# Order of the heads in the mixed rows of a two-pass attention backward kernel, and the steps at which their sums over wo are issued

## The chip, the cores and the metric

One core of one Trainium2 chip. The metric is the time of one execution on the device in microseconds (us); the kernel before took 892.82 us, the median of three runs (890.22 to 893.56). TensorE is PE in the profile's lines (PEld its weight loads), VectorE is DVE, ScalarE is ACT, GpSimd is POOL and SyncE is SP. SP and POOL issue the DMAs.

## The reference, cut to what matters

A decoding step of one pre-norm block, B = 2 sequences of one token, forward and backward. D = 640, 32 heads of 128, and a cache of 4096 keys and values per head.

```
q   = layernorm(x) @ wq                         # per head h: q[b,h], 128 wide
s   = K[b,h] @ q[b,h] * scale ; p = softmax(s)  # 4096 scores
o   = p @ V[b,h]                                # 128 wide
h1  = x + concat(o) @ wo
out = h1 + relu(layernorm(h1) @ w1) @ w2
# gradients of x, K, V, wq, wo, w1, w2 for a given grad_out. The two large ones, per (b, h):
go  = wo[h] @ g_h1[b]                           # 128 wide
gV  = outer(p, go)                              # 4096 x 128
dp  = V[b,h] @ go ; gs = p * (dp - dot(o, go)) * scale
gK  = outer(gs, q)                              # 4096 x 128
```

K and V are read (64 MB each in bf16), gK and gV of the same size are written. V is needed twice: for o, and after the MLP and its gradients for dp.

## The kernel before, in words

**First pass.** `p1_iter(i)`, one row i for each pair (b, h), i = 0 to 65, pipelined over three pairs: row i transposes and multiplies K of pair i (PE, `pair_transpose` and `pair_matvec`), forms the softmax weights of pair i-1 (`ep` on ACT) and K times these weights (`pk`, two halves on DVE, L523), and multiplies V of pair i-2 (`m_ps`, L516). It is a generator that yields eight times, k = 0 to 7; other work is put in at these points.

**Second pass.** `p2_iter(j)`, one head per j in the order of the list `turns`: V again (or still there) is transposed and multiplied by go to give dp, `gsp` (L956), and the outer products gV and gK, two halves each on DVE (L945), which are stored. `p2_tail` ends a head: gsp, two halves of gK, the store.

**The plan.** Rows i = 0 to 39 are first pass alone. From i = P2_AT = 40 each even row also starts a head j of the second pass, whose steps are dealt out to this row and the next odd one (MIXED, REST): j = 0 to 11 in rows 40 to 63, j = 12 and 13 in rows 64 and 65. In the even row stand the transposes of V and the first half of gV, in the odd one the second half of gV, gsp and both halves of gK. After row 65 the second pass runs alone, j = 14 to 63. In mixed rows the gradients are stored through the POOL queue (L1016, L1031), afterwards mostly through SP.

**Buffers and loads.** K, V and W tiles (W is V loaded again for the second pass), 1024 KB each, share 13 buffers of the pool `ld`; a few of them move to `g`, from which gK and gV are taken. The last six heads of each sequence are kept (KEPT = 6, 6): their V stays in its buffer from the first pass to the second, and no W is loaded. All loads are one queue, issued in order by `pump` on SP: K(i), V(i-2), then W of the head that the next row of the plan starts. A load takes the buffer that was given back earliest and waits on SP until its last readers are done; everything behind it waits too.

**The second pass's order for b = 0, before.** GROUPS[0] lists groups of heads: (26, 28), (28, 30), (30, 32), then (0, 8), (8, 16), (16, 24), (24, 26). `turns` follows it: the kept heads 26 to 31 are j = 0 to 5 (rows 40 to 51), the loaded heads 0 to 5 are j = 6 to 11 (rows 52 to 63), 6 to 25 follow.

**The sums over wo.** go of a head is 128 rows of wo times the gradient of h1, one DVE instruction each (`ttr`, L711, 0.82 us, output `rows<-wo_t,rows`). `go_group` makes the sums of one group, and then a chain of short instructions: two on DVE (L734, L736), `pair_rows` (four matmuls on PE, four copies on DVE, L395), the matmuls of `d_ps` (L741, L745), five more on DVE (L747 to L753). It is part of `middle_gen(0)`, which waits in the background queue `bg` and is advanced by `bg_step` after each yield of a row. `slot` says how many sums may be issued at this yield, a credit of 0.2 per yield (RATES[2]) is spent at 0.9 per sum and 0.5 per finished wait, and `wait(n)` lets n times `spread` yields pass (spread is 2 in mixed rows). In mixed rows a sum may be issued at k = 6 of every row and at k = 1 of rows without a head (the odd ones). Before a row with head j starts, `bg_until` issues at once whatever is still missing for that head's go.

Of the kernel before, what the change touches and what calls it, by code (L numbers as in the profile page):

```python
# [15 lines left out]
def kernel(  # L16
# [23 lines left out]
    _, H, Sk, Dh = A_k_cache.shape  # L40
# [13 lines left out]
    GH = 8  # L54
# [14 lines left out]
    def sm(name, dt, *dims):  # L69

        n = 1
        for d in dims:
            n *= d
        words = n if dt == FP32 else -(-n // 2)
        if name not in scr_at:
            scr_at[name] = scr_at.get(None, 0)
            scr_at[None] = scr_at[name] + words
            assert scr_at[None] <= NSCR, (name, scr_at[None])
        ap = scr[:, scr_at[name]:scr_at[name] + words]
        if dt != FP32:  # L80
            ap = ap.bitcast(dt)[:, 0:n]
        if len(dims) == 2:
            ap = ap.rearrange("p (a b) -> p a b", a=dims[0])
        return ap
# [79 lines left out]
    at_k = [1]  # L164
    spread = [1]
    forced = [False]

    def wait(n):

        end = step[0] + n * spread[0]  # L170
        while step[0] < end and not forced[0]:
            yield 0.0
        yield
# [196 lines left out]
    def wo_of(h, c0, c1):  # L370
        return wo_t[h // WH][:, (h % WH) * D + c0:(h % WH) * D + c1]
# [75 lines left out]
    KEPT = (6, 6)  # L447
    GROUPS = []
    for b in range(B):
        first = H - KEPT[b]  # L450
        if b == 0:
            GROUPS.append([(h, h + 2) for h in range(first, H, 2)] + [(h, min(first, h + GH)) for h in range(0, first, GH)])
        else:
            GROUPS.append([(first, H)] + [(h, min(first, h + WH)) for h in range(WH * ((first - 1) // WH), -1, -WH)])
    turns = [(b, h) for b in range(B) for h0, h1 in GROUPS[b] for h in range(h0, h1)]
    turn_of = {bh: j for j, bh in enumerate(turns)}
    kept = {(b, h) for b in range(B) for h in range(H - KEPT[b], H)}
    u_bank = [None]
# [249 lines left out]
    def ttr(in0, in1, acc, width, kc=128, junk=None):  # L708
        if junk is None:
            junk = junk_row  # L710
        nc.vector.tensor_tensor_reduce(out=junk[0:kc, 0:width], in0=in0, in1=in1, scale=1.0, scalar=0.0,  # L711
                                       op0=ALU.mult, op1=ALU.add, accum_out=acc)

    slot = [99]

    def turn():

        while slot[0] <= 0:
            yield 0.0
        slot[0] -= 1  # L720

    def one(src, b):
        return src[:, :, b]

    def go_group(b, h0, h1, hbc):

        hs = slice(h0, h1)
        n = h1 - h0
        go32 = sm("go32", FP32, GH)
        for k in range(n):  # L730
            yield from turn()
            ttr(wo_of(h0 + k, 0, D), hbc, go32[:, k:k + 1], D)
            yield 0.9
        nc.vector.tensor_copy(out=goc[:, hs, b], in_=go32[:, 0:n])  # L734
        pr = sm("pr", FP32, GH)
        nc.vector.tensor_tensor(out=pr[:, 0:n], in0=goc[:, hs, b], in1=OU[:, b, hs], op=ALU.mult)  # L736
        yield from wait(2)
        pair_rows(gom, goc, hs, slice(b, b + 1))
        yield from wait(2)
        d_ps = pst([128, 2, GH], FP32, "mid", "d_ps")  # L740
        nc.tensor.matmul(d_ps[:, 0, 0:n], lhsT=ones_f32, rhs=pr[:, 0:n], start=True, stop=True)  # L741
        for k in range(n):
            h = h0 + k
            MT, side, slot_mt = MTs.pop((b, h))
            nc.tensor.matmul(d_ps[:, 1, k:k + 1], lhsT=MT, rhs=goc[:, h, b:b + 1], start=True, stop=True)  # L745
            mt_free[side].append(slot_mt)
        nc.vector.tensor_scalar(out=negdot[:, hs, b], in0=d_ps[:, 0, 0:n], scalar1=-1.0, scalar2=None, op0=ALU.mult)  # L747
        ud = sm("ud", FP32, GH)
        nc.vector.tensor_tensor(out=ud[:, 0:n], in0=Uc[:, hs], in1=negdot[:, hs, b], op=ALU.mult)
        mg = sm("mg", FP32, GH)  # L750
        nc.vector.tensor_tensor(out=mg[:, 0:n], in0=d_ps[:, 1, 0:n], in1=rt[:, b, hs], op=ALU.mult)
        nc.vector.tensor_tensor(out=ud[:, 0:n], in0=mg[:, 0:n], in1=ud[:, 0:n], op=ALU.add)
        nc.vector.tensor_scalar(out=GQc[:, hs, b], in0=ud[:, 0:n], scalar1=SCALE, scalar2=None, op0=ALU.mult)  # L753
        for h in range(h0, h1):
            done.add(("go", b, h))
        yield
# [470 lines left out]
    P2_AT = H + 2 + M0_ITERS  # L1227
# [4 lines left out]
    i = j = 0  # L1232
# [51 lines left out]
    def p2_whole(j):  # L1284
        yield from p2_iter(j, 0)
        yield from p2_tail(j)
# [8 lines left out]
    for n, (i, j) in enumerate(plan):  # L1295
        all_go = all(("go", B - 1, h) in done for h in range(H))
        if i is None and plan[n - 1][0] is not None:
            pkp.release()
            big1 = tc.alloc_tile_pool(name="big1", bufs=1)
            for _ in range(2):  # L1300
                more_home("ld", big1)
            share(ld=KEPT[1] + 4, g=5)
        if ("w1", B - 1) in done:
            for t in range(NWO):
                if t not in late and all(("go", B - 1, h) in done for h in range(t * WH, min(H, (t + 1) * WH))) and \
                        (t < NWO - 1 or all_go):
                    late[t] = ("g", "g", "g", "q", "q", "q")[len(late)]
                    more_home(late[t], wop, f"wo{t}")
        lq, ll, lg = [sum(v == tag for v in late.values()) for tag in ("q", "ld", "g")]
        if fin is not None and not bg2 and not bg3:  # L1310
            share(ld=4, g=12 + 6 * (lq > 0))
        elif fin is not None and j >= H + KEPT[1] - 1:
            share(ld=4 + ll, g=7 + lg, f=3, q=2 + lq)
        if j is not None:
            while g2 is not None:
                p2_step()
            if j < NP1:
                bg_until(("go", *turns[j]))
            if i is not None and n + 1 < len(plan) and plan[n + 1][1] is None:
                g2 = p2_whole(j)  # L1320
            else:
                g2 = p2_iter(j, 0, 8 if i is None and j <= H else 0, nc.sync if i is None else None)
        if i is None and ("w1", 1) in done and fin is None:
            wts.release()
            fin = tc.alloc_tile_pool(name="fin", bufs=1)
            big2 = tc.alloc_tile_pool(name="big2", bufs=1)
            more_home("f", big2)
            banks.update(sps=[2, 3], o=[4, 5, 6])
            bg2.append(("fin", fin_gen(fin)))
            bg3.append(("gx", gx_gen(fin)))  # L1330
        if i == 12:
            bg.append(("ga", ga_gen()))
        if i == H + 2:
            banks["bc"].insert(0, banks["sps"].pop(0))
        elif i == P2_AT:
            banks["bc"].remove(7)
            banks["sps"].insert(0, banks["bc"][0])
            banks["bc"] = [7]
        rate = RATES[0 if i is not None and i <= H + 1 else 1 if j is None and i < P2_AT else
                     2 if i is not None else 3 if j <= H else 4]  # L1340
        if i is None:
            spread[0] = 2
            at_k[0] = 1
            k = 0
            while g2 is not None:
                p2_step()
                pump()
                slot[0] = int(k in ((1, 3, 5) if j <= H else (1, 4)))
                k += 1
                bg_step(0, rate)  # L1350
                bg_step(1, RATE2 * (0.4 if spreading[0] else 1.0))
                bg_step(2, RATE3)
            continue
        at = MIXED if j is not None else REST
        for k, _ in enumerate(p1_iter(i, i < H + 1, 0)):
            for _ in range(at.get(k, 0)):
                if g2 is not None:
                    p2_step()
            if k == 5:
                a_heads(i)  # L1360
            pump()

            spread[0] = 1 if i < P2_AT else 2
            at_k[0] = k
            if i >= P2_AT:
                slot[0] = int(k == 6 or (k == 1 and j is None))
            elif i > H + 1:
                slot[0] = {1: 2, 3: 1, 4: 1, 6: 1}.get(k, 0)
            else:
                slot[0] = int(k in (1, 6))  # L1370
            bg_step(0, rate)
            bg_step(1, 0.0)
        if i is not None and i in (H + 1, NP1 + 1):
            bg.append((f"m{i // H - 1}", middle_gen(i // H - 1)))
# [42 lines left out]
```

## Time and profile before

| | |
|---|---|
| median of three runs | 892.82 us (890.22 to 893.56) |
| the profiled execution | 893.07 us, its span 891.3 us |
| busy | PE 750.6 us (84%), DVE 685.0 (77%), ACT 487.1 (55%), POOL 155.8 (17%) |
| moved | 361.87 MB, mean 406 GB/s |
| loads | K 64, V 64, W 52 tiles of 1024 KB on SP |
| stores of gK and gV | 101 tiles on SP, 27 on POOL |
| sums over wo (L711, 128x640 from wo_t) | 64, 52.4 us, 818 ns each |
| chain that ended last, by engine | PE 44%, DVE 25%, DMA 11%, ACT 9%, issue 8% |

The page cuts the span into 40 slices of 22.3 us; digits are tenths, and the line of GB/s is what the DMA engines moved in each. A row of a timeline gives the start in us, the duration, the engine, the line in the kernel, the operation with output and inputs, and in brackets how long the engine idled before it and what released it. In the table of stretches the columns are busy time and number of instructions of PE, PEld, DVE, ACT and POOL, then the granted clock of PE, the DMA share and GB/s.

### The profile page before, as it was taken

What the parts mean: (1) busy time and instruction counts of PE and PEld (TensorE: products, weight loads), DVE (VectorE), ACT (ScalarE), POOL (GpSimd) and SP (SyncE); (2) the same over time, 40 slices, a digit from 0 to 9 for tenths busy, and PEclk for the clock granted to TensorE, in tenths of its full rate; (3) what the DMA queues carried; (4) which work ended last, traced back from release to release, by engine and by line L of the source; (5) the groups of instructions that cost most, each with busy time, mean ns of one, the idle gap of its engine ahead of it and who ended that gap; (6) DMA issues with size and microseconds to landing.
All of it is one profiled execution on the core that took longest, in us unless ns stands there. A gap on an engine that the chain in (4) does not pass through costs nothing.

```text
span 891.3 us, 24951 instructions
## 1 busy us (share of the span) xinstructions
PE 750.6 (84%) x10215; PEld 625.6 (70%) x10215; DVE 685.0 (77%) x1301; ACT 487.1 (55%) x1249; POOL 155.8 (17%) x264
## 2 busy tenths in 40 slices
PE   4999899999998989897986777878887887987880
PEld 4888787888887878787766666657666666655550
DVE  2666698877887887875868797788899489999751
ACT  1345343344655555564545777777566655656661
POOL 1344344343210010010111111011010001100200
PEclk9999899999999999998995555555566555556555
DMA  9999999999879999999999999999999999999996
GB/s 380 425 416 417 421 414 421 424 424 409 317 302 384 419 423 426 422 425 426 416 353 401 424 425 425 424 425 415 419 421 402 403 387 416 425 425 424 424 424 267
DMA packets 56115, 361.87 MB, mean 406 GB/s; under 512 B 5712, under 2 KB 11728, under 8 KB 15296
## 3 DMA queue, kind: packets, MB, share of 16 engines
q1 hardware_dynamic: 49096, 317.04, 86.6%
q0 software_dynamic: 6864, 43.22, 11.6%
q8 instruction: 80, 1.31, 0.5%
q14 instruction: 35, 0.29, 0.1%
q10 hardware_dynamic: 40, 0.01, 0.0%
HBM read 211.11 MB, written 149.13 MB: 404 GB/s over the span
## 4 chain that ended last, share of the span: by engine, by line
PE 44%; DVE 25%; DMA 11%; ACT 9%; issue 8%; SPq 0%; DVEq 0%; ACTq 0%; POOL 0%; POOLq 0%
PE t_ps L482 19%; PE m_ps L516 10%; DVE rows L711 7%; DVE gV L945 6%; DMA Vt<-in_A_v_cache_dram 6%; DVE gK L945 5%; ACT gV L1015 4%; PE s_ps L495 3%; DVE pk L523 3%; PE u_ps L545 3%; PE o_ps L1083 2%; PE dp_ps L495 2%; ACT t_sb L487 2%; DMA Kt<-in_A_k_cache_dram 2%; DMA out_dram<-gK 1%
## 5 line engine op out<-in xcount | busy, mean ns | idle before, releaser
L487 ACT COPY t_sb<-t_ps 128x512 f32<-128x512 f32 x479 | 273.9, 587 | 199.7 <-PE t_ps L482 196.4
L495 PEld LDWEIGHTS <-t_sb 128*128 128x128 bf16 x4096 | 180.0, 103 | 61.1 <-ACT t_sb L487 28.1
L482 PE MATMUL t_ps<-ident_f,Wt 128*128 128x128 f32 x832 | 199.2, 391 | 2.6 <-ACT t_sb L487 2.3
L523 DVE TENSOR_TENSOR pk<-Kt,ep 128x2048 bf16<-128x2048 bf16 x128 | 156.3, 1222 | 42.5 <-ACT ep L570 27.3
L516 PE MATMUL m_ps<-pk,Vt 128*128 128x129 bf16 x2048 | 172.5, 224 | 7.5 <-DMA Vt<-in_A_v_cache_dram 6.7
L482 PEld LDWEIGHTS t_ps<-ident_f,Wt 128*128 128x128 f32 x832 | 139.1, 203 | 32.1 <-issue 21.5
L482 PE MATMUL t_ps<-ident_f,Kt 128*128 128x128 f32 x1024 | 156.8, 286 | 3.7 <-DMA Kt<-in_A_k_cache_dram 3.1
L945 DVE TENSOR_TENSOR gK<-rb,gsp 128x2048 bf16<-128x2048 bf16 x128 | 153.0, 1221 | 6.7 <-DMA out_dram<-gV 4.9
L516 PEld LDWEIGHTS <-Vt 128*128 128x128 bf16 x2048 | 126.3, 99 | 38.0 <-issue 29.5
L945 DVE TENSOR_TENSOR gV<-rb,pp 128x2048 bf16<-128x2048 bf16 (+1 forms) x128 | 143.3, 1140 | 1.2 <-DMA out_dram<-gK 1.1
L482 PEld LDWEIGHTS t_ps<-ident_f,Kt 128*128 128x128 f32 x1024 | 113.4, 145 | 7.3 <-ACT t_sb L487 3.7
L495 PE MATMUL dp_ps<-gom,t_sb 128*128 128x2 bf16 x2048 | 96.3, 168 | 17.5 <-ACT t_sb L487 16.9
L533 POOL COPY pk<-ep 128x16 bf16<-128x16 bf16 x78 | 83.2, 1069 | 155.2 <-ACT ep L570 79.7
L495 PE MATMUL s_ps<-qm,t_sb 128*128 128x2 bf16 x2048 | 87.6, 164 | 1.2 <-DVE t_sb L485 1.2
L1089 ACT CAST ot<-o_ps 128x512 bf16<-128x512 f32 (+3 forms) x152 | 67.7, 492 | 4.1 <-DMA out_dram<-ot 2.9
L630 ACT CAST wo_t<-m_ps 128x128 bf16<-128x128 f32 x55 | 14.7, 266 | 78.0 <-PE m_ps L516 76.5
L983 POOL COPY pp<-P_bf 128x64 bf16<-128x64 bf16 x64 | 30.4, 476 | 145.2 <-DVE gV L945 140.7
L711 DVE CUSTOM_DVE_ANT_0 rows<-wo_t,rows 128x640 bf16<-128x640 bf16 x64 | 52.4, 818 | 1.9 <-ACT rows L688 1.8
L956 DVE SCALAR_TENSOR_TENSOR gsp<-dp_ps,negdot,P_bf 128x64 bf16<-128x64 f32 x64 | 17.9, 280 | 42.6 <-PE dp_ps L495 42.4
L1015 ACT ACTIVATE gV<-rb,pa 128x128 bf16<-128x128 bf16 x152 | 46.5, 392 | 6.2 <-DMA out_dram<-gK 6.2
L711 DVE CUSTOM_DVE_ANT_0 rows<-wqs,gqr 128x1024 bf16<-128x1024 bf16 x40 | 48.8, 1221 | 0.2
L981 ACT ACTIVATE rb<-dp_ps,rt 128x256 bf16<-128x256 f32 x64 | 30.2, 472 | 32.8 <-PE dp_ps L976 32.7
(205 smaller groups left out, 727.1 us busy)
## 6 DMA issues: line engine op xcount, KB each, us to landing
Kt<-in_A_k_cache_dram SPq DMA_DIRECT2D x64, 1024.0 KB, 18.5
Vt<-in_A_v_cache_dram SPq DMA_DIRECT2D x64, 1024.0 KB, 14.5
Wt<-in_A_v_cache_dram SPq DMA_DIRECT2D x52, 1024.0 KB, 13.8
out_dram<-gK SPq DMA_DIRECT2D x51, 1024.0 KB, 13.8
out_dram<-gV SPq DMA_DIRECT2D x50, 1024.0 KB, 13.4
out_dram<-gV POOLq DMA_DIRECT2D x14, 1024.0 KB, 10.3
out_dram<-gK POOLq DMA_DIRECT2D x13, 1024.0 KB, 10.2
out_dram<-ot POOLq DMA_DIRECT2D x6, 960.0 KB, 9.8
```

What stands on the lines that cost most here:

```text
L482: nc.tensor.transpose(t_ps[:, j, :], natf[:, 2 * cc:2 * cc + 2, :].rearrange("p c k -> p (c k)"), ident_f[:])
L487: nc.scalar.copy(out=t_sb[:], in_=t_ps[:])
L495: nc.tensor.matmul(dst[:, sc:sc + 2], lhsT=v[:, j, :, par], rhs=vecs[:, par, :], start=(par == 0), stop=(par == 1))
L516: nc.tensor.matmul(r["m"][:, 0:129], lhsT=r["V"][:, sc, :], rhs=r["pk"][sc // HALF][:, sc % HALF, 0:129], start=(sc == 0), stop=(sc == NSC ...
L523: nc.vector.tensor_tensor(out=p["pk"][k][:, :, 0:128].rearrange("p s (a two) -> p s a two", two=2), in0=p["K"][:, sl, :].rearrange("p s (a ...
L533: nc.gpsimd.tensor_copy(out=col, in_=e)
L711: nc.vector.tensor_tensor_reduce(out=junk[0:kc, 0:width], in0=in0, in1=in1, scale=1.0, scalar=0.0, op0=ALU.mult, op1=ALU.add, accum_out=acc)
L945: nc.vector.tensor_tensor(out=pairs_view(dst[:, sl, :]), in0=row.rearrange("p (a two) -> p a two", two=2)[:, None, :, :].to_broadcast([128 ...
L981: nc.scalar.activation(out=rb[:], in_=bank[:, 128:384], func=ACT.Copy, scale=rt[:, b, h:h + 1])
L983: nc.gpsimd.tensor_copy(out=pp[:], in_=P_bf[:, P_slot[(b, h)], :, None].to_broadcast([128, NSC, 2]))
L1015: nc.scalar.activation(out=gV[:, NSC - act + k, :], in_=c["rb"][:, 0:128], func=ACT.Copy, scale=pa[:, k:k + 1])
L1089: nc.scalar.copy(out=ot[0:kp, k, n0:n0 + nn], in_=o_ps[0:kp, 0:nn])
```

## The change

Three things in one diff.

The order of b = 0: kept and loaded heads alternate. `turns` begins 26, 0, 27, 1, 28, 2, 29, 3, 30, 4, 31, 5 (j = 0 to 11) and goes on with 6 to 25. The groups become (26, 28), (0, 2), (28, 30), (2, 4), (30, 32), (4, 8), (8, 16), (16, 24), (24, 26): nine instead of seven.

The sums: in mixed rows `slot` is 1 at k = 1, 3 and 4 of rows that carry a head, and 0 elsewhere.

The chain: in mixed rows both waits in `go_group` are one unit (two yields) instead of two, and after each the chain holds until k is 1, 2, 3 or 4 of some row.

```diff
         if b == 0:
-            GROUPS.append([(h, h + 2) for h in range(first, H, 2)] + [(h, min(first, h + GH)) for h in range(0, first, GH)])
+            late_kept = [(h, h + 2) for h in range(first, H, 2)]
+            early = [(0, 2), (2, 4), (4, GH)]
+            GROUPS.append([g for two in zip(late_kept, early) for g in two] +
+                          [(h, min(first, h + GH)) for h in range(GH, first, GH)])
...
     turns = [(b, h) for b in range(B) for h0, h1 in GROUPS[b] for h in range(h0, h1)]
+    stay = list(range(H - KEPT[0], H))
+    turns[0:2 * KEPT[0]] = [(0, h) for two in zip(stay, range(KEPT[0])) for h in two]
+    turns[2 * KEPT[0]:H] = [(0, h) for h in range(KEPT[0], H - KEPT[0])]
...
+    mixed = [False]
+
+    def early_step():
+
+        while mixed[0] and at_k[0] not in (1, 2, 3, 4) and not forced[0]:
+            yield 0.0
+
     def go_group(b, h0, h1, hbc):
...
-        yield from wait(2)
+        yield from wait(1 if mixed[0] else 2)
+        yield from early_step()
         pair_rows(gom, goc, hs, slice(b, b + 1))
-        yield from wait(2)
+        yield from wait(1 if mixed[0] else 2)
+        yield from early_step()
         d_ps = pst([128, 2, GH], FP32, "mid", "d_ps")
...
         if i is None:
+            mixed[0] = False
             spread[0] = 2
...
         at = MIXED if j is not None else REST
+        mixed[0] = i >= P2_AT
...
             if i >= P2_AT:
-                slot[0] = int(k == 6 or (k == 1 and j is None))
+                slot[0] = int(j is not None and k in (1, 3, 4))
```

## The prediction, on record before the result

> **What bounds the kernel now.** I read four views in this order: the page's slices, the table of 10 us stretches around the mixed rows, the timelines of the vector engine (DVE) and TensorE (PE) over one pair of rows, and the DMA issues of the SP queue.
>
> ```profile
> PEclk9999899999999999998995555555566555556555
> DMA  9999999999879999999999999999999999999996
> GB/s 380 425 416 417 421 414 421 424 424 409 317 302 384 419 423 426 422 425 426 416 353 401 424 425 425 424 425 415 419 421 402 403 387 416 425 425 424 424 424 267
> ```
>
> A slice is 22.3 us. Transfers run at about 424 GB/s nearly everywhere, so the kernel is bound by traffic, and time can only be won where the rate drops: slices 10 to 12 and 20 to 21. The mixed rows (i = 40 to 65) begin at about 249 us and end at about 461 us, so both dips touch them. In finer steps (the last two columns are the DMA share and GB/s):
>
> ```profile
> 250.00:260.00 10.00, 9.68 (x167) 8.65 (x165) 7.12 (x15) 6.80 (x20) 0.00 (x0) 1.00 0.82 309
> 260.00:270.00 10.00, 8.33 (x132) 6.75 (x129) 8.50 (x22) 5.70 (x15) 1.93 (x3) 0.98 0.73 266
> 270.00:280.00 10.00, 9.94 (x157) 8.73 (x154) 7.36 (x16) 4.58 (x13) 0.53 (x1) 0.85 0.99 382
> 280.00:290.00 10.00, 8.40 (x138) 7.45 (x136) 7.32 (x18) 5.37 (x14) 1.26 (x2) 1.00 1.01 397
> 290.00:300.00 10.00, 8.97 (x145) 7.86 (x144) 9.97 (x20) 6.21 (x17) 0.97 (x2) 1.00 1.02 424
> ...
> 440.00:450.00 10.00, 8.80 (x164) 7.81 (x162) 8.86 (x20) 4.57 (x15) 0.53 (x1) 0.99 0.98 388
> 450.00:460.00 10.00, 9.27 (x126) 7.52 (x123) 8.03 (x16) 5.39 (x14) 2.03 (x4) 0.83 0.92 329
> 460.00:470.00 10.00, 5.92 (x98) 5.16 (x95) 4.51 (x6) 4.22 (x9) 1.73 (x6) 0.88 0.99 378
> 470.00:480.00 10.00, 6.23 (x75) 5.96 (x74) 8.45 (x22) 4.64 (x13) 1.37 (x2) 0.50 1.01 375
> ```
>
> Each stretch loses 10 us x (424 - rate)/424. From 250 to 290 that is 2.7 + 3.7 + 1.0 + 0.6 = **8.1 us**; from 440 to 480 it is 0.8 + 2.2 + 1.1 + 1.2 = **5.3 us**. From 290 to 440 the rate is 421 to 427 but for one 412, so nothing is to be had there, even where PE waits for a transfer (it stands still for 0.3, 0.5 and 3.7 us between 404 and 415).
>
> Why do transfers pause at the start? The SP queue's longest waits are for buffers (80 us behind DVE's rmax, 80 us behind pk). All buffers are full, so a load starts only when computing frees one. The pace of that is DVE's and PE's. One pair of rows with its second-pass head, on DVE:
>
> ```profile
> 306.89 0.82 DVE L711 CUSTOM_DVE_ANT_0 rows<-wo_t,rows 128x640 bf16<-128x640 bf16 x1
> ...
> 309.16 0.82 DVE L711 CUSTOM_DVE_ANT_0 rows<-wo_t,rows 128x640 bf16<-128x640 bf16 x1
> ...
> 314.89 0.82 DVE L711 CUSTOM_DVE_ANT_0 rows<-wo_t,rows 128x640 bf16<-128x640 bf16 x1
> ...
> 319.51 0.18 DVE L604 RECIPROCAL rt<-s_ps 128x4 f32<-128x4 f32 x1 [1.89 <-PE s_ps L599]
> ```
>
> and on PE:
>
> ```profile
> 313.91 0.23 PE L561 MATMUL s_ps<-neg_ident,rmax 128*128 128x128 bf16 x1 [0.96 <-DVE rmax L618]
> ...
> 317.14 0.65 PE L482 MATMUL t_ps<-ident_f,Vt 128*128 128x128 f32 x4 [0.41 <-ACT t_sb L487]
> ```
>
> The three sums over wo (L711) stand in the odd row's 10 us (305.7 to 315.7), where DVE has no gap: two halves of gV, two of pk, two of gK, three sums. PE then waits for it (0.96 us, and 0.41 us behind a copy whose engine waited for DVE's nb). In the even row DVE idles instead (1.89 us in the last line, 0.47 + 0.26 + 0.27 besides).
>
> **The parts and their prices.** A tile is 1.049 MB, so 2.47 us at 424 GB/s. A pair of rows with a kept head moves 6 tiles (14.8 us), with a loaded head 7 (17.3 us), and the average is 16.07 us in either order. From one first half of gV to the next, pairs take 17.4, 16.2, 15.8, 15.9, 16.9 us before, mean 16.4.
>
> *Where the sums go (the slot line).* Three sums per pair as before, now all in the even row at k = 1, 3, 4. The odd row loses 3 x 0.74 to 0.82 = 2.3 us of DVE. The even row gains it; its gaps above hold 2.9 us, and the first of the sums delays only pk, which PE needs a row later. What comes back is PE's waiting, 0.41 + 0.96 + 0.41 = 1.8 us in a pair: 16.0 becomes 14.2 to 14.6 us where no chain runs.
>
> *Chains and groups.* Two more groups, each 1.65 us of DVE (441 to 451 us: 0.17 + 0.16 + 0.47 before and 0.15 + 0.16 + 0.15 + 0.16 + 0.23 after the matmuls) and some 0.6 us of PE, 4.5 us of work in all. Groups of two heads now fill the first four pairs, and their chains are held to k = 1 to 4, mostly of the odd row: copies 0.47 and the last five 0.8 us, so 1.3 of the 2.3 us freed there is spent again. So for pairs j = 0, 1, 2 I take 1.9 us (before, this pair had chain and sums together), 1.0 and 0.8 us: **3.7 us** sooner. All of it comes off the 8.1 us of pause, as each load there waits for computing. Bounds: 0 (releases set by something else) and 8.1.
>
> *Deadlines.* A pair earns 16 x 0.2 = 3.2 credits; a group of two costs 2 x 0.9 + 3 x 0.5 = 3.3. So head 0 is summed in i = 40 and done in 41, before j = 1 at i = 42 needs it; heads 28, 2 and 30 have a row or more to spare. I count on no forced chain. One would cost its 1.65 + 1.6 us in a row, once. In all, 29 sums and 7 groups cost 36.6 credits, 11.4 pairs, against 35.1 before, so the last group (24, 26) slides from i = 63 to about 65: up to 1.64 + 1.65 = 3.3 us of DVE where DVE is 80% busy and then idles 4.9 us for a store. I charge 1.1 of 0 to 3.3 us.
>
> *Order of heads.* The bytes stay. Loads for heads 0 to 4 enter the SP queue ten to two rows earlier, each ahead of the next K; the buffers of kept heads come free at i = 40 to 60 instead of 40 to 50. Every pair still frees as many buffers (a loaded head's own is freed where a kept one's was), so the number of loads does not change; K and V slip back by one place from i = 42, two from 46, three from 50, and regain them by 60.
>
> ```profile
> 289.77 0.33 SPq L503 DMA_DIRECT2D Kt<-in_A_k_cache_dram  x1
> 290.19 0.38 SPq L503 DMA_DIRECT2D Vt<-in_A_v_cache_dram  x1
> 297.79 0.33 SPq L503 DMA_DIRECT2D Kt<-in_A_k_cache_dram  x1
> ```
>
> Counting back from the last K, the first of these is the K of i = 47, used at 306.15: a lead of 16.4 us. Two places later it goes out at 297.79: 8.4 us. By the same count the K of 46 keeps 6.3 us, the V of 44 8.0, of 45 9.2. Loads issued in 250 to 300 us land in 6.8 us (K, median) and 11.6 (V). So the lead is about what a landing takes. I price the shift at 0, since two or three loads and a store are then still under way and keep the engines busy while PE waits; the upper end is the slower rival's.
>
> *The end.* Before, loads outrun computing until the buffers are used up, then heads 0 to 5 come at 17.3 us a pair and PE waits at 404 to 415. Afterwards computing is late: the last K is issued at 410.5 and used at about 441, and transfers pause at 440 to 460 for lack of free buffers. Pairs 10 and 11 without the sums are 1.2 to 1.3 us shorter each, **2.5 us** of the 5.3. Bounds 0 and 5.3.
>
> **The sum:** -3.7 - 2.5 + 1.1 = -5.1 us. The profiled execution took 893.07 us (span 891.3 and 1.8 around it), 0.25 above the median of the three runs; 893.07 - 5.1 = **888.0 us**. After 480 us the rate is 415 to 426 but for two stretches, and all shifts with the start.
>
> A rule speaks against this. The Trainium skill, DMA: Bandwidth & Descriptors, Specifications, puts a core's share of HBM at about 358 GB/s. By it a kept pair's 6.29 MB would take 17.6 us (an estimate from that page), more than computing, and no order could gain: 893. The trace holds 424 GB/s for 150 us; the measurement decides.
>
> **Rivals.**
> 1. *Traffic anyway.* The releases at the start do not come sooner: the chains of four small groups, or credits that hold sums and chains to later steps than the change says, eat the 2.3 us. For it: DVE is at 7.1 to 8.5 of 10 there, not full. Against it: the ungapped odd row. Left are 2.5 at the end less 1.1: 891.6 us. Chance 0.26.
> 2. *The lead runs out* (slower). From i = 43 to 50 computing waits for tiles while too few loads are under way, because kept heads hold buffers until i = 60. It decides from the point where a landing takes longer than the mean lead of 8.2 us; two loads and two stores at 2.47 us are 9.9. Six rows (of j = 1, 3, 5) at 1.7 us are 10 us: 893.1 - 5.1 + 10 = 898 us. For it: V's 11.6 us. Against it: K's 6.8, and the queue would have to empty. Chance 0.20.
> 3. *Nearly all pauses go.* Computing at 14.4 us a pair keeps up with the last K and both pauses close but for the charge: 893.1 - 13.4 + 1.1 = 881 us. Chance 0.12.
>
> **How the numbers follow.** The forecast has 0.42 (its own range 885 to 889). Faster by over 0.5% (4.5 us, about what a measurement of this kernel can tell from no change) holds it and rival 3: 0.54. Within 0.5% is rival 1: 0.26. Slower is rival 2: 0.20. The range 881 to 898 leaves out the far halves of rivals 2 and 3, some 0.16.
>
> **What would show it.** Right: 250 to 290 us loses about 4 us, 440 to 480 less than 4; L711 falls in even rows at 0.82 us, no longer between gV and gsp; odd rows take about 8.5 us from rmax to nb; W loads alternate from 249 us on; no PE wait of over 1 us for V or K. Wrong: PE waits for K or V between 270 and 340 with the rate below 400 (rival 2); the rate at 250 to 290 as before (rival 1); a run of L711 and d_ps in front of a head's rb, a forced chain.

## The result: slower by 0.7%

| | before | changed |
|---|---|---|
| median (six runs each) | 890.89 us (888.93 to 893.56) | 897.70 us (895.73 to 898.17) |
| ratio, 95% interval | | 1.0068 (1.0051 to 1.0085) |
| profiled execution, span | 893.07 us, 891.3 us | 897.90 us, 896.1 us |

The forecast was 888.0 us. What happened is the second rival, to which the prediction gave 0.20 and 898 us.

The changed kernel's page, the same three lines as before:

```profile
PEclk9999899999998998998995555555656555556555
DMA  9999999999789999999999999999999999999996
GB/s 378 424 417 418 422 415 420 423 425 406 295 299 384 374 405 359 423 425 425 424 406 401 419 425 425 425 425 416 418 425 414 408 386 419 424 426 424 424 425 256
```

The dip at slices 10 to 12 is still there, and slices 13 to 15 are new: 374, 405, 359 where it was 419, 423, 426. In stretches of 10 us of the changed kernel (last columns: granted clock of PE, DMA share, GB/s):

```profile
250.00:260.00 10.00, 9.68 (x152) 8.57 (x152) 7.77 (x25) 6.42 (x17) 0.00 (x0) 1.00 0.85 301
260.00:270.00 10.00, 9.41 (x161) 8.12 (x158) 9.61 (x19) 6.74 (x19) 1.45 (x3) 1.00 0.77 283
270.00:280.00 10.00, 7.98 (x124) 7.15 (x117) 6.47 (x16) 4.02 (x12) 0.53 (x1) 0.84 1.01 393
280.00:290.00 10.00, 9.79 (x138) 8.22 (x137) 7.63 (x18) 5.38 (x14) 0.77 (x2) 0.82 1.00 372
...
300.00:310.00 10.00, 7.07 (x95) 6.35 (x95) 6.20 (x15) 4.11 (x11) 0.77 (x2) 0.83 0.98 372
310.00:320.00 10.00, 9.09 (x165) 8.10 (x163) 8.10 (x22) 5.91 (x17) 0.53 (x1) 1.00 0.93 327
...
340.00:350.00 10.00, 9.45 (x147) 8.89 (x148) 3.83 (x10) 3.88 (x10) 0.00 (x0) 0.74 0.90 351
350.00:360.00 10.00, 9.34 (x155) 8.24 (x152) 8.96 (x21) 6.70 (x20) 1.31 (x3) 1.00 0.97 350
...
450.00:460.00 10.00, 8.70 (x135) 7.44 (x131) 8.88 (x23) 3.64 (x12) 0.77 (x2) 0.83 1.01 422
```

With the prediction's 10 us x (424 - rate)/424 for each stretch, and stretches a little above 424 GB/s counted against the rest, the transfers lose (the last row in stretches of 20 us):

| us lost in | before | changed |
|---|---|---|
| 220 to 250 (rows ahead of the change's) | 6.2 | 7.5 |
| 250 to 290 | 8.1 | 8.2 |
| 290 to 440 | 0.1 | **7.1** |
| 440 to 500 | 5.4 | 2.4 |
| 500 to 880 | 5.1 | 4.0 |

That is +4.3 of the 4.8 us between the two spans. The first row is not the change's: at 220 to 230 the clock was granted at 0.83 in this execution, and e13 below, whose rows there are those of the kernel before, has the same clock and loses 7.5 us. The row 290 to 440 is the change's.

Inside the worst place, three views of the changed kernel. First the loads that SP issued:

```profile
327.09 0.33 SPq L509 DMA_DIRECT2D Kt<-in_A_k_cache_dram  x1
328.24 0.33 SPq L509 DMA_DIRECT2D Vt<-in_A_v_cache_dram  x1
328.62 1.10 SPq L509 DMA_DIRECT2D Kt<-in_A_k_cache_dram  x1
334.83 0.33 SPq L509 DMA_DIRECT2D Vt<-in_A_v_cache_dram  x1
335.26 0.44 SPq L509 DMA_DIRECT2D Kt<-in_A_k_cache_dram  x1
348.24 0.33 SPq L509 DMA_DIRECT2D Vt<-in_A_v_cache_dram  x1
```

then what PE waited for:

```profile
336.12 1.06 PE L488 MATMUL t_ps<-ident_f,Kt 128*128 128x128 f32 x8 [2.00 <-DMA Kt<-in_A_k_cache_dram]
340.55 1.05 PE L522 MATMUL m_ps<-pk,Vt 128*128 128x129 bf16 x8 [3.31 <-DMA Vt<-in_A_v_cache_dram]
```

then the clock and the rate in stretches of 5 us:

```profile
335.00:340.00 5.00, 1.12 (x9) 0.92 (x9) 2.67 (x8) 1.07 (x2) 0.78 (x2) 0.83 1.03 431
340.00:345.00 5.00, 4.45 (x42) 4.39 (x43) 1.23 (x1) 2.06 (x6) 0.00 (x0) 0.50 1.00 423
345.00:350.00 5.00, 5.00 (x107) 4.50 (x106) 2.61 (x9) 1.82 (x4) 0.00 (x0) 0.99 0.80 280
```

Read together: PE stands still for a K (2.0 us), then for a V (3.3 us). By the chain, that V is the one issued at 328.24; it landed 12.3 us later. While PE waits, and then runs at half clock for five microseconds, nothing gives a buffer back, so SP issues no load for 13 us (335.26 to 348.24): 12.5 us of this the profile puts down to DVE's `pk` (L529), whose second half ends at 348.22 and gives a K's buffer back. The loads under way last until about 345, and then the transfers pause. The same shape stands at 273.5 to 284.1 (PE waits 1.96 us, no load for 10.5 us) and at 300.8 to 310.2 (2.19 us; 9.4 us).

The kernel before has such a wait as well, 3.7 us at 411, then a clock of 0.52 and no load from 410.5 to 423.3:

```profile
410.50 0.44 SPq L503 DMA_DIRECT2D Kt<-in_A_k_cache_dram  x1
423.31 0.33 SPq L503 DMA_DIRECT2D Vt<-in_A_v_cache_dram  x1
...
414.84 1.05 PE L516 MATMUL m_ps<-pk,Vt 128*128 128x129 bf16 x8 [3.71 <-DMA Vt<-in_A_v_cache_dram]
...
415.00:420.00 5.00, 5.00 (x46) 4.94 (x45) 1.22 (x1) 2.41 (x7) 0.00 (x0) 0.52 1.01 424
```

Its rate stayed at 424: loads issued in 385 to 425 take about 20 us to land (medians 19.7 for V, 23.2 for K, 20.6 for W), so enough were queued to last.

### The profile page after: what moved, and what is told of

Its sections match the earlier page's. It is cut to its first block, busy times and chain, and to the rows that moved or that the text cites. A ratio compares the mean times of both kernels' runs of the same rounds, so it can differ in the third digit from the quotient of the medians.

```text
span 896.1 us, 24989 instructions
## 1 busy us (share of the span) xinstructions
PE 753.9 (84%) x10227; PEld 628.8 (70%) x10227; DVE 689.5 (77%) x1323; ACT 487.3 (54%) x1249; POOL 153.6 (17%) x264
## 3 DMA queue, kind: packets, MB, share of 16 engines
q0 software_dynamic: 6864, 43.22, 11.6%
## 4 chain that ended last, share of the span: by engine, by line
PE 44%; DMA 27%; DVE 11%; ACT 10%; issue 4%; SPq 0%; DVEq 0%; ACTq 0%; POOL 0%; POOLq 0%
PE t_ps L488 20%; DMA Vt<-in_A_v_cache_dram 13%; PE m_ps L522 10%; DMA out_dram<-gV 7%; DMA Wt<-in_A_v_cache_dram 5%; ACT t_sb L493 4%; ACT gV L1030 3%; PE s_ps L501 3%; DVE gV L960 3%; PE u_ps L551 3%; DVE gK L960 3%; PE dp_ps L501 2%; PE o_ps L1098 2%; DVE rows L717 2%; DVE pk L529 2%
## 5 line engine op out<-in xcount | busy, mean ns | idle before, releaser
L488 PE MATMUL t_ps<-ident_f,Wt 128*128 128x128 f32 x832 | 201.6, 394 | 3.3 <-DMA Wt<-in_A_v_cache_dram 2.6
L529 DVE TENSOR_TENSOR pk<-Kt,ep 128x2048 bf16<-128x2048 bf16 x128 | 156.3, 1222 | 40.6 <-ACT ep L576 31.7
L488 PEld LDWEIGHTS t_ps<-ident_f,Wt 128*128 128x128 f32 x832 | 141.2, 205 | 30.2 <-issue 22.2
L998 POOL COPY pp<-P_bf 128x64 bf16<-128x64 bf16 x64 | 27.6, 434 | 143.3 <-DVE gV L960 140.0
## 6 DMA issues: line engine op xcount, KB each, us to landing
Kt<-in_A_k_cache_dram SPq DMA_DIRECT2D x64, 1024.0 KB, 17.4
Vt<-in_A_v_cache_dram SPq DMA_DIRECT2D x64, 1024.0 KB, 14.6
out_dram<-gK SPq DMA_DIRECT2D x51, 1024.0 KB, 15.3
```

The lines of the kernel that those rows point to most:

```text
L488: nc.tensor.transpose(t_ps[:, j, :], natf[:, 2 * cc:2 * cc + 2, :].rearrange("p c k -> p (c k)"), ident_f[:])
L529: nc.vector.tensor_tensor(out=p["pk"][k][:, :, 0:128].rearrange("p s (a two) -> p s a two", two=2), in0=p["K"][:, sl, :].rearrange("p s (a ...
L998: nc.gpsimd.tensor_copy(out=pp[:], in_=P_bf[:, P_slot[(b, h)], :, None].to_broadcast([128, NSC, 2]))
```

## The experiments

Two theories. **Lead**: kept heads hold their buffers until row 60 and the early W loads take places ahead of K and V, so too few loads are under way; all of the loss comes from the order, and a buffer more or less in those rows decides. **Steps**: sums in the even rows, chains held to early steps, or the two added chains cost the time. Ratios are against the kernel before on the same chip, with 95% intervals. "Pause" is what the transfers lose in 290 to 440 us of the run's profiled execution, summed as above. Differences in us are worked out from the ratio unless they are said to be of medians; in the e3 to e17 diffs, a comment behind a line names the runs that have it.

### e1: the order alone

```diff
-                slot[0] = int(j is not None and k in (1, 3, 4))
+                slot[0] = int(k == 6 or (k == 1 and j is None))
...
-        yield from wait(1 if mixed[0] else 2)
-        yield from early_step()
+        yield from wait(2)
```

(against the changed kernel; the last edit twice)

> The new order and its nine groups alone; sums and chains at the steps of the kernel before. Theory (the lead of the loads runs out, because kept heads hold buffers until row 60 and early W loads take places ahead of K and V): the whole loss is in here, and the steps gave some of it back; +7 to +11 us against the kernel before, PE waits for V of 10 us or more and a rate below 400 GB/s somewhere in 290 to 360 us. Rival (the sums in the even rows and the chains held to early steps cost the time): within 2 us of the kernel before.

897.90 us, 1.0070 (1.0044 to 1.0097), +6.2 us; pause 6.3 us, PE waits for V 7.1 us in 250 to 480. The loss is all in the order with its groups; the steps gave nothing back (897.7 with them). The theory had the sign and the place; its range began at 7, and it asked for 10 us or more of PE waits for V.

```profile
300.00:310.00 10.00, 8.77 (x122) 8.20 (x123) 3.50 (x8) 3.97 (x10) 0.82 (x2) 0.66 0.81 306
310.00:320.00 10.00, 9.20 (x152) 8.06 (x150) 9.55 (x23) 5.38 (x16) 0.53 (x1) 1.00 0.95 328
```

The new hole (306 and 328 GB/s) with a clock of 0.66, here with the old steps.

### e2 and e10: the steps alone

e2 is the changed kernel with the old `GROUPS` and `turns`. e10 also has the old waits, so only this line differs in effect from the kernel before:

```diff
-                slot[0] = int(k == 6 or (k == 1 and j is None))
+                slot[0] = int(j is not None and k in (1, 3, 4))
```

> The old order and its seven groups, with the new steps for sums and chains. Theory: faster than the kernel before by 1 to 4 us, because the odd rows lose 2.3 us of DVE work and the pauses of the transfers at 250 to 290 us (8.1 us) and 440 to 480 us (5.3 us) shrink. Rival (the steps cost the time): slower by 4 us or more.

> Old order and groups, the sums in the even rows, but the chains at their old waits and free to stand at any step. Theory: what the steps give comes from the sums leaving the odd rows, so within 1.5 us of the run with both (890.3 us). If holding the chains matters, this run is slower by 2 us or more.

e2: 890.26 us, 0.9987 (0.9961 to 1.0013). e10: 889.36 us, 0.9980 (0.9964 to 0.9995), the only version whose interval lies below 1, and by little. Steps are not the cause, and holding the chains makes no difference that shows. In e10 the odd row takes 8.5 us from rmax to nb, two of DVE's reductions (303.65 to 312.12), instead of 10.0, and pairs last 14.6 and 14.8 us (ACT's rb, once per head, at 282.67, 297.26, 312.01). PE waits for V 11.4 us in e2 and 10.8 in e10 (250 to 480 us), about as long as in the changed kernel (12.2), and yet the pauses are 0.3 and 0 us: a wait by itself costs no transfers. The loss in 250 to 290 us is 6.9 us (6.7 in e2) against 8.1, but e4, e5, e8 and e13 below, with the old steps, also lose 6.7 to 6.9 there, so this is not shown to come from the steps. The first 20 us of the mixed rows in e10:

```profile
250.00:260.00 10.00, 9.68 (x154) 8.48 (x151) 8.05 (x24) 6.21 (x18) 0.00 (x0) 1.00 0.84 310
260.00:270.00 10.00, 9.41 (x153) 8.30 (x152) 9.16 (x19) 6.90 (x19) 1.45 (x3) 1.00 0.74 280
```

Here 6.1 us are lost, 6.4 before. PE is busy 9.4 to 9.7 of 10 us, so freeing DVE does not shorten this pair. It also has little to move: the first gV is stored at 262, and between 251.4 and 266.3 SP issues one load, as row 40 hands K's buffer to the pool of gK and gV.

### e5: nine groups, old order

```diff
-            GROUPS.append([(h, h + 2) for h in range(first, H, 2)] + [(h, min(first, h + GH)) for h in range(0, first, GH)])
+            GROUPS.append([(h, h + 2) for h in range(first, H, 2)] + [(0, 2), (2, 4), (4, GH)] +
+                          [(h, min(first, h + GH)) for h in range(GH, first, GH)])
```

> The nine groups of the change, but the heads in the old order (kept ones first) and the old steps: the two more chains by themselves. Theory (lead of the loads): within 2 us of the kernel before. Rival (the two more chains carry the loss that the run with the order alone showed, 6 to 7 us): 5 us or more slower.

891.92 us, 1.0037 (1.0011 to 1.0063); pause 0.7 us. The median is 1.8 us over, the ratio 3.3; the runs fall in two heaps, around 891 and 897. The added chains cost something between 1 and 5 us in this run, but e16 below has the same nine groups at 1.0011 (0.9989 to 1.0034). So a part of 0 to 3 us may be theirs, not the loss.

### e3, e12 and e14: buffers in the changed kernel; e4 and e13: controls

The rule by which a buffer goes from loads to gK and gV, with `owned["g"] < 3` in both kernels:

```diff
-        give(c["W"], "g" if j < H and j != 1 and owned["g"] < 3 else None)
+        give(c["W"], "g" if j < H and j != 1 and owned["g"] < 2 else None)                      # e3; e4 on the kernel before
+        give(c["W"], "g" if j < H and j != 1 and owned["g"] < (2 if j < 8 else 3) else None)    # e12; e13 on the kernel before
+        give(c["W"], "g" if j < H and j != 1 and owned["g"] < 4 else None)                      # e14
```

> The changed kernel, but only two buffers move to the pool of gK and gV in the mixed rows instead of three, so one more is left for loads from row 44. Theory: the lead grows by one place where the transfers paused (300 to 360 us, 7.0 us in all), 3 to 6 us come back: about 892 to 895 us. Rival (steps, or the two more groups): within 1 us of the changed kernel. Two buffers for gK and gV might be too few: then DVE waits for a store in the mixed rows, and the run is slower.

> Control: the kernel before with the same one more buffer for loads from row 44. Theory: its transfers run at 424 GB/s from 290 to 440 us already, so the buffer only lengthens the lead; within 1.5 us of the kernel before. If any added buffer is worth 3 us or more here too, the gain of the run before it says nothing on the order.

> The changed kernel; the third buffer for gK and gV is taken from the loads only from head j = 8 (row 56) on, not at row 44. Theory: as with two buffers, the pause in 290 to 440 us goes from 7.1 us to 1 to 2 us, and the end of the mixed rows, where two buffers made DVE wait for stores, is as in the changed kernel: 890 to 894 us. If the lead is not the cause: 896 to 899 us.

> Control: the kernel before with the same late third buffer. Its transfers have no pause in 290 to 440 us to fill: within 1.5 us of the kernel before.

> The changed kernel with a fourth buffer for gK and gV, so one less for loads from row 48 on. Theory: the lead shrinks by one more place, the pause in 290 to 440 us grows from 7.1 to 10 us or more, 900 us or more. If buffers are not short there: within 1.5 us of the changed kernel.

| | buffers for gK, gV | time | ratio | pause |
|---|---|---|---|---|
| e3, changed | 2 | 894.57 | 1.0048 (1.0024 to 1.0072) | 1.2 |
| e12, changed | 2, then 3 from row 56 | 892.83 | 1.0026 (0.9999 to 1.0053) | (5.6) |
| changed | 3 | 897.70 | 1.0068 (1.0051 to 1.0085) | 7.1 |
| e14, changed | 4 | 903.54 | 1.0149 (1.0103 to 1.0196) | 15.0 |
| e4, before | 2 | 894.28 | 1.0032 (1.0008 to 1.0056) | 0 |
| e13, before | 2, then 3 | 892.87 | 1.0014 (0.9989 to 1.0039) | 0 |

The changed kernel and these runs were measured on different chips, so they are compared by their ratios. One buffer less for loads (e14): 7 us and 8 us of pause more. The stretches of e14:

```profile
340.00:350.00 10.00, 8.00 (x92) 7.02 (x91) 4.01 (x12) 3.90 (x10) 0.00 (x0) 0.61 0.74 313
350.00:360.00 10.00, 9.34 (x173) 8.24 (x171) 8.17 (x20) 6.04 (x17) 0.53 (x1) 1.00 0.86 272
```

One more gave 1.8 us (e3, whose interval overlaps that of the changed kernel), and 3.7 us where it is lent only to row 56 (e12). In the old order the same edits gain nothing and two buffers cost 2.9 us (e4; I had expected within 1.5: there DVE waits 10.8 us for stores, 6.0 before). So e3's net is probably a gain of the lead less that price. The bracketed pause of e12 is of an execution that was the slowest of its eleven (899.14 us), so it does not stand for the median; there my expectation of 1 to 2 us was not shown.

### e8, e9, e11, e15: other orders

```diff
+    turns[0:12] = [(0, h) for h in (26, 27, 28, 0, 29, 1, 30, 2, 3, 31, 4, 5)]    # e8 old steps, e9 new steps
+    turns[0:12] = [(0, h) for h in (26, 27, 0, 28, 1, 29, 2, 30, 3, 31, 4, 5)]    # e11 old steps, e15 new steps
```

(their nine groups stand in the order of need, and heads 6 to 25 follow)

> The old steps and an order between the two: 26, 27, 28, 0, 29, 1, 30, 2, 3, 31, 4, 5, with nine groups in the order of need. K and V slip back by one or two places from row 46 to 57 (7 places times heads, against 15 in the change, 0 before). Theory: the loss grows with these places; about half of that of the order alone (6.2 us): 2 to 4 us over the kernel before, the pause in 290 to 440 us 1 to 4 us against 6.3. Rival (any mixing of the order costs, or the groups): as the order alone, 5 to 7 us.

> The same order between the two with the new steps for sums and chains. Theory: the run before it less about what the steps give (0 to 2 us); pauses of 1 to 4 us in 290 to 440 us: 889 to 893 us. Faster than the old order with the new steps (890.3 us) only if evening out the loads is worth more than the lead that it takes.

> Old steps, nine groups, alternating as in the change but two heads later: 26, 27, 0, 28, 1, 29, 2, 30, 3, 31, 4, 5. K and V slip by one or two places (10 places times heads; 15 in the change with a pause of 6.3 us in 290 to 440 us, 7 in the order that began the loads at row 46 with 0.5 us). Theory (a lead that is enough or not enough): one more buffer is free when the first loaded head comes, so the pause is 1 to 3 us and the time 1 to 4 us over the run with nine groups in the old order (891.9). Rival (alternation as such, whatever the lead): as the order alone, 897 to 899 us.

> The order that alternates from row 44 (26, 27, 0, 28, 1, 29, 2, 30, 3, 31, 4, 5) with the new steps. If the lead is all that the order costs: 890 to 893 us, the pause in 290 to 440 us below 3 us. If alternation costs something else as well: 896 us or more, as with the old steps (897.2).

e8: 893.36 us, 1.0039 (1.0009 to 1.0069), pause 0.5. e9: 891.50 us, 1.0005 (0.9982 to 1.0029), pause 0.5. Loads that begin at row 46 leave no hole: e8 is level with e5, the same groups without mixing. It is not half of the loss, as I had expected from counting places: either enough loads are under way or not.

e11: 897.21 us, 1.0070 (1.0040 to 1.0100); e15: 896.82 us, 1.0065 (1.0041 to 1.0088). Both miss: putting the first loaded head one place later than the change, at row 44, costs as much as the change. In e15 the reason shows, a pause of 6.6 us (321, 334 and 338 GB/s at 290, 300 and 330). In e11 the profile has only 1.8 us there, but 8.0 in 440 to 500, and 3.2 more than before ahead of row 40 (0 to 250 us), where nothing was edited. That profile does not explain its median.

### e16 and e17: the order with the lead given back

The order of e1 (old steps), and that of e15 (new steps), each with e12's late third buffer.

> The full alternation with the old steps and the third buffer for gK and gV taken only from row 56. If the lead is all: the pause in 290 to 440 us goes from 6.3 to 1 to 2 us and the time from 897.9 to 892 to 894 us. If not, within 2 us of 897.9.

> Alternation from row 44, new steps, third buffer from row 56: no pause of over 1.5 us in 290 to 440 us, 889 to 891 us, so no better than the old order with the sums in the even rows (889.4). Below 887 us, evening out the loads is worth something once the lead is there.

e16: **890.43 us, 1.0011 (0.9989 to 1.0034)**, pause 0.8. The full alternation of heads with nine groups costs nothing that can be measured once one more buffer serves the loads up to row 56 (expected were 892 to 894 us): by the ratios 5.3 us of e1's 6.2 are back, and what is left, 1.0 us, may be anything from -1 to 3. The same buffer gained nothing in the old order (e13).

```profile
300.00:310.00 10.00, 8.31 (x133) 7.78 (x134) 5.13 (x15) 3.88 (x10) 1.26 (x2) 0.83 1.00 424
310.00:320.00 10.00, 9.19 (x145) 8.04 (x144) 9.75 (x25) 5.93 (x17) 0.76 (x2) 1.00 1.01 387
```

PE still waits for V in e16 (1.04, 0.68 and 1.83 us between 276 and 302, the last with the clock down), but the rate holds: what decides is whether loads are still under way meanwhile. e17: 893.80 us, 1.0031 (1.0009 to 1.0052), pause 3.2, a miss against an expected 889 to 891 us and 1.5. With the new steps PE arrives earlier at a V (wait 3.73 us at 283, clock 0.55 for five microseconds, no load from 283.1 to 295.6, 242 GB/s in 295 to 300). Neither is faster than e10, so no gain from evening out the loads shows here.

## Why the prediction was wrong, step by step

**What binds.** Right: traffic at 424 GB/s, and time is lost only where the rate drops. Of the 4.8 us between the two spans, 4.3 are in what the transfers lose.

**Where the sums go.** Right on DVE: three sums in the even row, none between gV and gsp, and in e10 8.5 us in the odd row and pairs of 14.6 and 14.8 us (forecast 14.2 to 14.6); in the changed kernel, which waits for loads, the first five pairs take 15.1 to 20.7 us (by rb). The term of 3.7 us, which was to come back in 250 to 290, is not to be seen: nine profiles with the new steps lose 6.7 to 8.7 us there (mean 7.4), eight with the old steps 6.7 to 8.1 (mean 7.1), and the 8.1 of the kernel before that the prediction read is the highest of these eight (its clock fell to 0.50 at 270, and that of e4, e5, e8 and e13 did not). I had credited 1.9 us of the gain to the first pair, reading it from the spacing of gV (17.4 us), which reaches into the second. By rb the first pair lasts 15.3 us in the kernel before and 15.3 in e10; PE fills it, and it has few loads to issue.

**The end.** 440 to 500 us lost 2.4 instead of 5.4 us in the changed kernel: about the gain of 2.5 that was forecast. e10 shows 2.2, e2 5.0, so one profile settles nothing, but the same nine profiles with the new steps have a mean of 2.8 us (1.3 to 5.1), the eight with the old steps one of 5.2 (3.5 to 8.0): 2.4 us less. This term held on average; that it comes from the shorter pairs 10 and 11 was not tested.

**Chains and groups.** No chain was forced. The charge of 1.1 us lies within what e5 and e16 leave (0 to 3 us).

**Order of heads.** This is the step that failed. The prediction worked out the leads (6.3 to 9.2 us), said that they are about what a landing takes, and priced the shift at 0, "since two or three loads and a store are then still under way and keep the engines busy while PE waits". The leads were right: from issue to the moment at which PE began to wait, the four long waits of the changed kernel between 270 and 345 us (1.96 to 3.31 us) have 7.0 to 9.0 us. The price was not: e1 measures +6.2 us for the order and its groups. Between 290 and 345 us V took 10.9 us to land and K 11.9 (medians), PE waited, the buffers stayed taken, no load went out for 9 to 13 us, and the loads under way ran out before that: the transfers lost 7.1 us. That e16 wins nearly all of it back with one buffer, which gains nothing in the old order, and that e14 doubles the pause by taking one, shows that the loss comes through the buffers left for loads. The number of loads per pair did not change, as I argued; but a load is issued only when computing moves, and computing moves only when a load lands, so where the loads under way end before the next buffer is given back, a lead shorter than a landing stops both.

**The second rival** had this mechanism, its place (PE waits for K or V between 270 and 340, the rate below 400) and its turning point (a landing above the mean lead of 8.2 us). Its price was put together from six waits of 1.7 us; PE's waits for K and V in 250 to 360 us are 9.8 us in five, and what counts is the pause behind them, 7.1 us, plus little gained elsewhere. Its number came close by parts that were not all right. The evidence for it, V's landing of 11.6 us, was in the prediction; I gave more weight to K's 6.8, which was measured in a stretch (250 to 300 us) whose mean rate was 355 GB/s.

**The rule on 358 GB/s** (the Trainium skill, DMA: Bandwidth & Descriptors, Specifications) played no part: the kernel before holds 421 to 427 GB/s in all but one stretch from 290 to 440 us, and the changed kernel 423 to 427 from 360 to 450.

## What to carry to other kernels

When loads wait for buffers, read two numbers in the trace before moving work among them: from a load's issue to its first use (the lead), and from issue to landing at the rate you expect to reach, not at the rate of a half-idle stretch. A change that spreads traffic evenly but holds buffers longer takes from the lead, and a lead shorter than the landing stops computing; the transfers stop too if the loads under way end before the next buffer is given back. A buffer given to another use and back at another row is a cheap test of it.

## What the runs showed that was not expected

PE's clock fell behind the long waits, and the work after them ran slower. In the changed kernel PE stood still for 1.96 us at 274.5, and the granted clock was 0.50 from 277 to 283 us; it was 0.50 in 340 to 345, after waits of 2.00 and 3.31 us, and there eight m_ps took 1.05 us. In e16 a wait of 1.83 us was followed by 0.50 in 302 to 304, while one of 1.04 us left it at 1.00, and eight m_ps behind it took 0.64 us. But the length of one wait does not settle it: a wait of 1.20 us in the kernel before was followed by 0.50 in 270 to 273, one of 1.19 us at the same place in e5 was not, and in the changed kernel the clock stood at 0.50 in 223 to 225 although the profile has PE busy from 216 on. The Trainium skill, TensorE: Matmul & The Clock Gate, Part 1 (the HAM clock gate), says that the clock falls to half after an idle window of about 3.4 us, and has no states between. The half is what the traces show, and in rows of 1 us other values stand only where it changes; the 3.4 us are not: waits of 1.83 and 1.96 us, and less, went with it, and the measurement decides. What sets the clock here stays open.

Identical rows ahead of the change cost 6 to 9 us of lost transfers at 220 to 250 us: 7.5 to 8.6 in the profiles whose clock dipped to 0.85 or less at 220, as in the changed kernel and e13 (7.5 both), and 5.8 to 7.5 in the others (6.2 before). Differences of 1 to 2 us between single profiles are of this size; only the intervals of many runs tell them apart.

What stays open: why e11 is as slow as the full alternation although its profile shows little pause, why e5's runs fall in two heaps 6 us apart, and why e8's spread over 11 us. Nor is it shown how much of the lost lead comes from the kept heads' buffers and how much from the places that W's loads take in the queue: e16 and e14 change the number of buffers, not the queue.
